# Two transformer layers on one core: norm transposes by DMA, and a reordered first and last stage

## The chip, the cores and the metric

The kernel runs on one core of a Trainium2 chip. The metric is device time in microseconds for one launch. The core has TensorE (matrix products, shown as PE, with its weight loads as PEld), VectorE (DVE), ScalarE (ACT), GpSimd (POOL) and SyncE (SP), which here only issues DMAs. TensorE writes to PSUM[...]; everything else lives in SBUF.

## The reference

The input is 2048 rows of 512 values in bf16. Attention block A and MLP block B are applied twice, with the same weights both times:

```python
x = A_x
x = x + _A_ref(_layernorm(x, axis=-1), A_wqkv, A_wo)
x = x + _B_ref(_layernorm(x, axis=-1), B_w1, B_w2)
x = x + _A_ref(_layernorm(x, axis=-1), A_wqkv, A_wo)
x = x + _B_ref(_layernorm(x, axis=-1), B_w1, B_w2)
return x
```

`_A_ref` is softmax attention without a mask: 32 heads of 16 values, scores scaled by 1/4, each of 2048 queries against 2048 keys, then a product with `wo` (512 x 512). `_B_ref` is `relu(x @ w1) @ w2` with 1792 hidden values. `_layernorm` has no gain or offset; its epsilon is 1e-5.

## The kernel before, in words

**Tiling.** Rows are held as 16 tiles of 128 (`x_t`). A chunk of queries is 512 rows (four tiles) in layer 0. In layer 1 there are two such chunks and then four of 256 rows (`chunks`, L444 to L448), so that less is left after the last one. The last chunk is called LAST, number 5 of layer 1.

**Attention.** Heads have only 16 values, so K and Q lie transposed, four groups of 32 partitions to a tile of heads T. The score matmul at L1302 takes one of the four groups, 32 partitions deep. Each group of 32 holds two heads, and `q_masked` (L624) makes two copies of Q, each with the other head's rows put to zero (the mask `e`). A segment is one chunk, one T and one `e`: sixteen key blocks by four groups. A block is one key block and one group by 512 queries (two key blocks where a chunk has 256). Blocks go in slots of three: a slot fills the three banks of one of the two score tiles `ps_s0` and `ps_s1`, in turn. ScalarE then takes the exponential of the slot in one instruction (L1311), and TensorE multiplies the result with V (L901) into one bank, `ps_o`. V carries a column of ones, so the sums for the softmax come out with the product.

**Pairs.** In some slots the third block does not go to ScalarE but to VectorE (`dve_block`, L991). Two such blocks, two slots apart, are a pair. VectorE makes `exp` from a line (`lin`, L995), the bits of its mantissa (`step`, L1036) and a cube (L1047, L1051), and TensorE multiplies all three with V. ScalarE's instruction then has 1024 columns in place of 1536.

**The planner.** The order of all instructions is made when the program is built. A loop over slots (from L1173) keeps model clocks for TensorE (`now_pe`), VectorE (`now_dve`) and ScalarE (`exp_end`). Other TensorE work is cut into groups of pieces (Q, K, V, Wo, the two MLP products, and the norms' transposes), kept in `work` and `urgent`. `fill_pe` (L307) puts pieces in front of a slot's scores as far as the pace of the stage asks and the model time allows. All of these groups share the one bank `ps_f` outside the first and the last stage. VectorE's tasks lie in `dve_q`, each with a cost and with keys it depends on; `mark` notes when a result is there by the model, with a lag if it comes from GpSimd or a DMA. `run_until` forces what is needed at once. A pair is begun (L1195 to L1220) only if VectorE's queue allows it (L1207, L1208), if the last pair's second half is done, and in layer 0 only if the last V block exists, except for one pair at a time (L1200). Spare TensorE time is filled with repeats of the scores (L1297).

**Norms.** `ln_rows` (L524) makes the tasks: statistics for each tile (L465, L466), then the start of a reciprocal root on VectorE (three small operations, L473 to L480), three Newton steps on GpSimd (L498 to L503), then the apply for each tile (L507). `ln_groups` (L549) makes four TensorE transposes for a tile (L516) into `ps_f`, and VectorE copies the bank to `xnT` (L558). K, V, Q and the first MLP product read `xnT`. There are 16 such norms with 58 tiles. The first norm of all and that of LAST are written out by hand, with the root wholly on VectorE (`ln_rstd` in four parts).

**The end of a segment** (`finish_segment`, L793). The sums are copied from `ps_o` to `u` (L823). For most segments they then go by DMA to a small tile `c` (L828), are inverted (L847), go back (L848), are spread over the partitions by GpSimd's DMA (L850) or a shuffle (L860), and multiplied in (L836). Only the last two segments are divided directly from `u` (`direct`, L869), with the shuffle, then a reciprocal (L873) and a product for each 128 rows.

**First stage.** Eighteen dummy products (L1069) run while the first x tiles arrive. Then come the norm, four transposes with copies that alternate between VectorE and ScalarE (L1092), K for T = 0 and Q for T = 0 with their evacuations, and two V blocks, whose copies are on ScalarE (L1116). Products rotate through seven banks, so K falls in bank 1 of `ps_s1`, Q in its bank 2 and the first V block in `ps_f`. The first slot's scores use `ps_s1`.

**Last stage** (from L1340). When the last segment is done, `run_all` finishes the rest of the MLP of chunk LAST-1 but for its first row tile. Then the rows of LAST get x and seven of the eight head pairs' products with Wo (L1368), the last pair's division and product, a copy by ScalarE (L1375), the norm, the transposes, then the MLP with W1 blocks loaded through the four buffers of `w1buf`, and the store. `half_part(0)` (L1402) does the row tile of LAST-1 that had been kept back.

Of the kernel before, what the change touches and what calls it, by code (L numbers as in the profile page):

```python
# [19 lines left out]
EPS = 1e-5  # L20
RSQRT_SEED = 0x5F3759DF
# [3 lines left out]
def kernel(  # L25
# [55 lines left out]
    RSTD_LAG = 5000.0  # L81
    AHEAD = (8.0, 8.0)
# [72 lines left out]
    stats = [sb([P, nc.vector.BN_STATS_DIM], FP32, f"stats{n}") for n in range(2)]  # L155
# [46 lines left out]
    def bank():  # L202
        if ending[0]:
            bank_no[0] += 1
            return (ps_f[:], ps_s[0][:, 0, :], ps_s[1][:, 0, :])[bank_no[0] % 3]
        if not wide[0]:
            return ps_f[:]
        n = bank_no[0] % 7
        bank_no[0] += 1
        in_bank[0] = (2, 0) if n == 6 else (n // W, n % W)  # L210
        if n == 6:
            return ps_f[:]
        return ps_s[n // W][:, n % W, :]
# [247 lines left out]
    def ln_stats(tag, tt, i):  # L461
        if tag not in ln_seq:
            ln_seq.append(tag)
        st = stats[i % 2]
        nc.vector.bn_stats(out=st[:], in_=x_t[tt][:])  # L465
        nc.vector.bn_aggr(out=mv[ln_n(tag)][:, i, :], in_=st[:])  # L466

    def ln_rstd(tag, part):

        n = ln_n(tag)  # L470
        a, y, t1 = va_[n], ya_[n], ta_[n]
        if part == 0:
            nc.vector.tensor_scalar(  # L473
                out=a[:], in0=mv[n][:, :, 1], scalar1=EPS, scalar2=None, op0=ALU.add
            )
            nc.vector.tensor_scalar(
                out=t1[:].bitcast(I32), in0=a[:].bitcast(I32), scalar1=1, scalar2=None,
                op0=ALU.logical_shift_right,
            )
            nc.vector.tensor_scalar(  # L480
                out=y[:].bitcast(I32), in0=t1[:].bitcast(I32), scalar1=-1.0,
                scalar2=float(RSQRT_SEED), op0=ALU.mult, op1=ALU.add,
            )
            return
        nc.vector.scalar_tensor_tensor(
            out=t1[:], in0=y[:], scalar=-0.5, in1=y[:], op0=ALU.mult, op1=ALU.mult
        )
        nc.vector.tensor_mul(out=t1[:], in0=t1[:], in1=a[:])
        nc.vector.scalar_tensor_tensor(
            out=y[:], in0=t1[:], scalar=1.5, in1=y[:], op0=ALU.add, op1=ALU.mult  # L490
        )

    def ln_newton(tag):

        n = ln_n(tag)
        a, y, t1 = va_[n][:], ya_[n][:], ta_[n][:]
        for _ in range(3):
            nc.gpsimd.tensor_mul(out=t1, in0=y, in1=y)  # L498
            nc.gpsimd.tensor_mul(out=t1, in0=t1, in1=a)
            nc.gpsimd.tensor_scalar(  # L500
                out=t1, in0=t1, scalar1=-0.5, scalar2=1.5, op0=ALU.mult, op1=ALU.add
            )
            nc.gpsimd.tensor_mul(out=y, in0=y, in1=t1)  # L503
# [20 lines left out]
    def ln_rows(tag, tt, n, i):  # L524

        if tag not in ln_seq:
            ln_seq.append(tag)
        at_tag = ln_seq.index(tag)
        prev = ln_seq[at_tag - 1]
        rows_of_prev = chunks[prev[1:]][1]  # L530
        before_that = ln_seq[at_tag - 2] if at_tag > 1 else None
        old = each(chunks[before_that[1:]][1], "xn", before_that) if at_tag > 1 else []
        if ("st", tag, i) not in made:
            task(830, lambda: ln_stats(tag, tt + i, i), [("st", tag, i)], old)
        if i == n - 1:

            def rstd():
                ln_rstd(tag, 0)
                ln_newton(tag)
                mark(("rs", tag, 3), lag=RSTD_LAG)  # L540

            task(500, rstd, [("rs", tag, 3)], each(n, "st", tag) + old)
            for k in range(n):
                task(
                    325, lambda k=k: ln_apply(tag, tt + k, k), [("xn", tag, k)],
                    [("xT", prev, k)] * (k < rows_of_prev) + [("rs", tag, 3)],
                )

    def ln_groups(tag, dst, at_column, n, war):  # L549
        groups = []  # L550
        for i in range(n):

            def piece(i=i):
                pt = ln_transpose(tag, i)

                def fin():
                    a = at_column + i * P
                    nc.vector.tensor_copy(out=dst[:, :, a : a + P], in_=pt)  # L558
                    mark(("xnT", tag, i))

                put_evac(342, fin)

            groups.append(
                group([(1.3, piece)], [("xT", tag, i), ("xnT", tag, i)], [("xn", tag, i)] + war)
            )
        return groups
# [91 lines left out]
    def load_w1(n):  # L658

        if n < len(chunks) * NF:  # L660
            ft = n % NF
            nc.sync.dma_start(
                out=w1buf[n % NW1][:],
                in_=B_w1[:, ft * P : (ft + 1) * P].rearrange("(c p) f -> p c f", p=P),
            )
            mark(("w1", n), "pe", 4000.0)
# [65 lines left out]

    def rest_of_chunk(l, j):

        b = before(l, j)
        xj, a, w = columns(l, j)
        n = w // P
        war_h = each(chunks[b][1], "z", *b) if b else []
        work[0:0] = [o_group(l, j, i) for i in range(n)] + ln_groups(
            ("ln2", l, j), xnT[xj], a, n, []  # L740
        )
        gs = [h_group(l, j, ft, war_h) for ft in range(0, NF, QS // w)]
        gs += [z_group(l, j, i) for i in range((l, j) == (1, LAST - 1), n)]
        if l == 0:
            gs += ln_groups(("ln1", 1, j), xnT[j], 0, TPC, [])
            gs.append(k_group(1, 0, j))
            gs += [v_group(1, kb) for kb in range(j * TPC, (j + 1) * TPC)]
            gs += [k_group(1, T, j) for T in range(1, 4)]
        return gs
# [43 lines left out]
    def finish_segment(sg, last):  # L793
# [37 lines left out]
        musts.append((77 + 1.045 * width, now_pe[0] + PE_TO_DVE, copy))  # L831
# [37 lines left out]
        def direct(i):  # L869
            if i == 0:  # L870
                spread()
            a = i * P
            nc.vector.reciprocal(out=r[:, a : a + P], in_=r[:, a : a + P])  # L873
            mul(a, P)
# [36 lines left out]
    def v_ready(sg, t):  # L911

        found = []
        done = [
            (p, x) for p in pairs if p["sg"] is sg
            for x in p["mms"] if x[4] in made and at([x[4]], "pe") <= t
        ]
        slots = [s for s in pend if s["ready"] <= t]
        for g in range(4):
# [3 lines left out]
                for s in slots for x in s["blocks"] if x[0] is sg and x[2] == g  # L923
# [42 lines left out]
    def force_v():  # L966
# [6 lines left out]
        if not found:  # L973
            run_until(next(x[4] for p in pairs if p["sg"] is sg for x in p["mms"]))
            found = v_ready(sg, 1e18)
        for home, _, _ in found:
            for s in pend:
                if s["blocks"] is home:
                    t = max(t, s["ready"])
            for p in pairs:  # L980
                if p["mms"] is home:
                    t = max(t, *(at([f[1][4]], "pe") for f in found if f[0] is home))
# [89 lines left out]
    idle_matmuls(18)  # L1072
# [12 lines left out]
    for part in range(4):  # L1085
        ln_rstd(tag, part)
# [3 lines left out]
    for i in range(TPC):  # L1090
        pt = ln_transpose(tag, i)
        copy = nc.scalar.copy if i % 2 else nc.vector.tensor_copy  # L1092
        uses(copy(out=xnT[0][:, :, i * P : (i + 1) * P], in_=pt), in_bank[0], "xnT")
        mark(("xnT", tag, i))
        idle_matmuls(1)
    for i in range(3):
# [13 lines left out]
    b = plain(q_mms(0, 0, 0))  # L1110
    for e in range(2):
        uses(q_masked(0, b, e), in_bank[0])
    mark(("q", 0))
    for kb in range(2):
        b = plain(v_mms(kb))
        uses(nc.scalar.copy(out=v_out(0, kb), in_=v_in(b)), in_bank[0])  # L1116
        mark(("v", 0, kb))
    work.extend(v_group(0, kb) for kb in range(2, TPC))
    for j in range(1, NQS):
# [4 lines left out]
        work.extend(ln_groups(tag, xnT[j], 0, TPC, []))  # L1124
# [40 lines left out]
    now_pe[0] = 12000.0  # L1165
    now_dve[0] = 13400.0
    exp_end = {-1: 13600.0, 0: 13600.0}
# [5 lines left out]
    while units:  # L1173
# [155 lines left out]
        for sg, kb, g in now:  # L1329
            run_until(("v", sg["l"], kb))  # L1330
# [9 lines left out]
    while seg_at[0] < len(segs):  # L1340
        force_v()
        run_dve(0.0, musts)
    ending[0] = True
    run_all()
    ending[0], wide[0] = False, True
# [22 lines left out]
    for i in rows:  # L1368
        add(banks[i], ident[:], x_t[tt + i][:], True, False)
        for t in range(NT - 1):  # L1370
            add(banks[i], ot[t][:, part(i)], wo[:, t // 2, :], False, False)
    for i in rows:
        last_steps[0](i)
        add(banks[i], ot[NT - 1][:, part(i)], wo[:, (NT - 1) // 2, :], False, True)
# [3 lines left out]
    for step in range(4):  # L1378
        ln_rstd(tag, step)
    for i in rows:  # L1380
        ln_apply(tag, tt + i, i)

# [26 lines left out]
    for ft in range(NF + 1):  # L1409
        if ft < NF:  # L1410
            n = (l * NQS + j) * NF + ft
            b = more[ft % 4]
            for c in range(NDC):
                add(
                    b, w1buf[n % NW1][:, c, :], xnT[NQS - 1][:, c, at_column : at_column + width],
# [10 lines left out]
            load_w1(n + NW1)  # L1426
# [6 lines left out]
    for i in rows:  # L1433
        copy = nc.vector.tensor_copy if i % 2 else nc.scalar.copy
        uses(copy(out=x_t[tt + i][:], in_=at_bank(banks[i])), banks[i])
        nc.sync.dma_start(
# [32 lines left out]
```

The softmax here doesn't subtract the row's maximum and nothing guards it: scores larger than these inputs give would overflow.

## Time and profile before

| | before |
|---|---|
| time, median of 3 runs | 1613.98 us (1613.9 to 1615.33) |
| span of the profiled run | 1611.5 us |
| ScalarE, VectorE, TensorE busy | 97%, 93%, 90% |
| exponentials (L1311) | 1366, 1554.8 us |
| of these with 1024 columns | 662 |
| pairs on VectorE (L1047) | 331 |
| first exponential starts, last one ends | 16.81 us, 1577.8 us |
| copies of transposes (L558) | 58, 24.3 us |
| W1 loads | 140 of 128 KB |

A line of the groups of instructions has the line of the kernel, the engine, the operation, the tile written and the tiles read, the shapes and the number; after the bar come the busy time and the mean of one in ns; after the next bar, how long the engine had been idle before them, and what ended most of that. TensorE overlaps its products, so sums of its durations overstate its load. VectorE's instructions overlap a little too: the next one often starts some 0.1 us before the recorded end of the one before.

### The profile page before, as it was taken

The page shows a single profiled execution, that of the slowest core. Times are in us where ns is not written, and L with a number is a line of the kernel's source. Part 1 is how long each engine was busy: PE and PEld are TensorE (multiplying, and loading weights), DVE is VectorE, ACT ScalarE, POOL GpSimd, SP SyncE. Part 2 cuts the span into 40 slices and gives each one's busy share as a digit, 9 for nine tenths or more (in the row PEclk, how much of TensorE's full clock was granted, in tenths as well). Part 3 has the DMA queues.
Part 4 walks back from the last instruction along what each step waited for, and adds up shares of the span by engine and source line. Part 5 has one row for each costly group of instructions (what it writes and reads, how often), then busy time and mean ns, then how long its engine had stood idle before and what let it go on. Part 6 is the DMA issues. An engine that isn't in the chain of part 4 may idle for free.

```text
span 1611.5 us, 35252 instructions
## 1 busy us (share of the span) xinstructions
PE 1451.6 (90%) x14667; PEld 508.9 (32%) x14863; DVE 1496.8 (93%) x3007; ACT 1566.0 (97%) x1387; POOL 93.8 (6%) x279
## 2 busy tenths in 40 slices
PE   8888888999989999899998998888989999899997
PEld 3222222322222222222222222222333333344444
DVE  7669999999999999999898998999999999999994
ACT  6999999999999999999999999999999999999993
POOL 2000001001010011000100000001001010010100
PEclk9999999999999999999999999999999999999999
DMA  5000000210002100021000100000210111121223
GB/s 164 1 1 2 2 2 10 46 28 12 5 18 45 21 15 9 12 47 25 9 1 17 31 1 1 2 3 9 44 30 16 26 29 36 22 48 36 47 46 73
DMA packets 113889, 39.97 MB, mean 25 GB/s; under 512 B 103328, under 2 KB 111264, under 8 KB 113728
## 3 DMA queue, kind: packets, MB, share of 16 engines
q1 hardware_dynamic: 101696, 26.21, 7.1%
q0 software_dynamic: 10688, 10.18, 3.4%
q8 instruction: 116, 1.90, 0.5%
q10 hardware_dynamic: 1344, 1.31, 0.2%
q14 instruction: 45, 0.37, 0.1%
HBM read 24.38 MB, written 2.10 MB: 16 GB/s over the span
## 4 chain that ended last, share of the span: by engine, by line
ACT 78%; PE 11%; DVE 7%; issue 3%; DMA 1%; ACTq 0%; DVEq 0%
ACT e L1311 78%; PE ps_s L1302 4%; PE ps_o L901 3%; PE ps_f L434 3%; DVE lin L995 2%; DVE step L1036 1%; PE ps_s L1365 1%; DVE cube L1047 1%; DVE cube L1051 1%; DVE stats L465 0%; DVE ht L682 0%; DVE q L625 0%; DVE ot L836 0%; DVE x L708 0%; DMA c<-u 0%
## 5 line engine op out<-in xcount | busy, mean ns | idle before, releaser
L1311 ACT ACTIVATE e<-ps_s 128x1024 bf16<-128x1024 f32 (+1 forms) x1366 | 1554.8, 1367 | 6.6 <-PE ps_s L1302 4.7
L1302 PE MATMUL ps_s<-q,ktp 32*128 32x512 bf16 (+1 forms) x6060 | 601.2, 341 | 106.7 <-ACT e L1311 84.7
L901 PE MATMUL ps_o<-e,vaug 128*32 128x512 bf16 (+1 forms) x4284 | 494.7, 345 | 11.3 <-DVE u L823 4.8
L995 DVE TENSOR_SCALAR lin<-ps_s 128x512 int16<-128x512 f32 x662 | 452.6, 686 | 35.8 <-PE ps_s L1302 30.4
L1302 PEld LDWEIGHTS <-ktp 32*128 32x128 bf16 x6060 | 189.9, 91 | 504.5 <-issue 375.6
L1036 DVE TENSOR_SCALAR step<-lin 128x1024 int16<-128x1024 int16 x662 | 262.9, 420 | 3.3 <-PE ps_o L901 0.6
L901 PEld LDWEIGHTS <-vaug 128*32 128x32 bf16 x6004 | 161.5, 94 | 302.2 <-issue 291.5
L1047 DVE TENSOR_TENSOR cube<-step 128x1024 f16<-128x1024 bf16 x331 | 225.9, 685 | 2.7
L1051 DVE TENSOR_TENSOR cube<-cube,lin 128x1024 bf16<-128x1024 f16 x331 | 225.5, 682 | 0.0
L901 PE MATMUL ps_o<-step,vaug 128*32 128x512 bf16 (+1 forms) x836 | 143.2, 340 | 0.3 <-issue 0.3
L901 PE MATMUL ps_o<-cube,vthird 128*32 128x512 bf16 (+1 forms) x788 | 138.2, 337 | 0.6 <-issue 0.3
L901 PE MATMUL ps_o<-lin,vaug 128*32 128x512 bf16 (+1 forms) x836 | 127.4, 338 | 4.1 <-DVE u L823 2.8
L434 PE MATMUL ps_f<-xnT,w 128*128 128x512 bf16 (+1 forms) x446 | 116.9, 345 | 5.6 <-issue 2.5
L434 PE MATMUL ps_f<-w,ht 128*128 128x512 bf16 x334 | 104.8, 384 | 5.6 <-issue 4.3
L850 POOL DMA_DIRECT2D r<-u x52 | 37.5, 721 | 1165.9 <-DVE step L1036 424.3
L434 PE MATMUL ps_f<-xnT,wqkv 128*128 128x512 bf16 (+1 forms) x288 | 82.3, 359 | 6.4 <-issue 2.5
L682 DVE TENSOR_SCALAR ht<-ps_f 128x512 bf16<-128x512 f32 x103 | 70.7, 687 | 3.2 <-PE ps_f L434 3.0
L434 PE MATMUL ps_f<-wo,ot 128*128 128x512 bf16 x206 | 65.4, 384 | 3.0 <-issue 1.9
L625 DVE TENSOR_SCALAR q<-ps_f,qmask 128x512 bf16<-128x512 f32 (+1 forms) x102 | 64.8, 661 | 3.1 <-PE ps_f L434 3.0
L434 PEld LDWEIGHTS <-w 128*128 128x128 bf16 x504 | 39.1, 97 | 60.0 <-issue 50.6
L836 DVE SCALAR_TENSOR_TENSOR ot<-u,mask,r 128x512 bf16<-128x512 f32 (+2 forms) x82 | 51.3, 627 | 1.1
L901 PEld LDWEIGHTS <-vthird 128*32 128x32 bf16 x788 | 39.8, 95 | 32.8 <-issue 30.1
(91 smaller groups left out, 609.8 us busy)
## 6 DMA issues: line engine op xcount, KB each, us to landing
w<-in_B_w_dram SPq DMA_DIRECT2D x140, 128.0 KB
r<-u POOLq DMA_DIRECT2D x25, 256.0 KB, 7.1
r<-u POOLq DMA_DIRECT2D x27, 128.0 KB, 4.5
out_dram<-x SPq DMA_DIRECT2D x16, 128.0 KB
x<-in_A_x_dram SPq DMA_DIRECT2D x14, 128.0 KB
w<-in_B_w_dram SPq DMA_DIRECT2D x1, 1792.0 KB
wqkv<-in_A_wqkv_dram ACTq DMA_DIRECT2D x2, 512.0 KB
c<-u SPq DMA_DIRECT2D x48, 8.0 KB
```

Source lines behind the costliest of these rows:

```text
L434: nc.tensor.matmul(out, lhsT, rhs, start=i % k == 0, stop=i % k == k - 1)
L625: return nc.vector.tensor_scalar(out=qbuf[n % 2][e][:, 0:w], in0=b, scalar1=qmask[e][:, 0:1], scalar2=None, op0=ALU.mult,)
L682: nc.vector.tensor_scalar(out=out, in0=sums, scalar1=0.0, scalar2=None, op0=ALU.max)
L836: nc.vector.scalar_tensor_tensor(out=ot[t][:, at_column + a : at_column + a + w], in0=u[:, a : a + w], scalar=mask[e][:, 0:1], in1=r[:, a ...
L850: nc.gpsimd.dma_start(out=r[:, 0:width], in_=bass.AP(tensor=sums.tensor, offset=sums.offset, ap=[list(sums.ap[0]), [0, 32], [1, width]],),)
L901: nc.tensor.matmul(ps_o[32 * g : 32 * g + 32, 0 : sg["w"]], values[:, 4 * sg["T"] + g, 2 * e : 2 * e + 32], rhs, start=g not in sg["begun" ...
L995: first = nc.vector.tensor_scalar(out=lin[which][:, half * QS : (half + 1) * QS], in0=src, scalar1=EXP_BIAS, scalar2=0.0, op0=ALU.add, op1 ...
L1036: nc.vector.tensor_scalar(out=stair, in0=line, scalar1=keep, scalar2=put, op0=ALU.bitwise_and, op1=ALU.bitwise_or,)
L1047: (609, lambda: nc.vector.tensor_mul(out=power, in0=mantissa, in1=mantissa)),
L1051: (609, lambda: nc.vector.tensor_mul(out=power.bitcast(BF16), in0=power, in1=line.bitcast(BF16))),
L1302: nc.tensor.matmul(b[:, a : a + sg["w"]], kt[32 * g : 32 * g + 32, kc : kc + P], qbuf[sg["n"] % 2][sg["e"]][32 * g : 32 * g + 32, 0 : sg[" ...
L1311: ex = nc.scalar.activation(out=eb[:, 0 : place[m]], in_=b[:, 0 : place[m]], func=ACTF.Exp, scale=1.0 / (LOG2E * UNIT),)
```

## The change: what it does and what it is for

**Transposes by DMA.** A norm's apply is followed by a DMA from SyncE's queue that transposes the tile from `xnbuf` straight to `xnT`. TensorE's transposes and VectorE's copies are gone for all 16 planned norms. The planner counts the result as there `X_LAG` = 4000 ns after the apply. The purpose is to take work from VectorE, TensorE and the bank `ps_f`.

**Norm arithmetic.** The statistics are gathered first and aggregated with the seed of the root. The seed takes two VectorE operations for three. Where the root is wholly on VectorE, a cubic step with a gain and one Newton step take the place of three Newton steps.

**First stage.** There are 24 dummy products for 18. The first two copies of transposes go to ScalarE and the last two to VectorE. Two tiles of the next norm get their statistics ahead of Q, where it was three. The first V block goes between Q's two masks and is copied by VectorE; the second becomes planned work. The slot loop no longer forces the V blocks of a slot: a product with V is picked only when its V block exists, by two new tests in `v_ready` and `force_v`. The loop's starting clocks are new numbers.

**Last stage.** The last segment's sums are spread and divided straight from `ps_o`, ahead of the leftover MLP of chunk LAST-1, and the rows' products with Wo follow at once. The W1 blocks of the last chunk are loaded ahead: four in `w1buf` and ten in buffers of layer 0's K that are no longer in use. The last stores go from two queues.

The diff, cut to its core:

```diff
@@ finish_segment
-        musts.append((77 + 1.045 * width, now_pe[0] + PE_TO_DVE, copy))
+        if last:
+            sums_wait[0] -= 1
+        else:
+            musts.append((77 + 1.045 * width, now_pe[0] + PE_TO_DVE, copy))
...
         def direct(i):
+            source = ps_o if last else u
             if i == 0:
-                spread()
+                nc.vector.stream_shuffle(
+                    out=r[:, 0:width], in_=source[:, 0:width], mask=[lane] * 32
+                )
@@ ln_seed, in place of the first part of ln_rstd
+        for i in range(rows):
+            nc.vector.bn_aggr(out=mv[n][:, i, :], in_=stats[n][:, i, :])
+        nc.vector.tensor_scalar(
+            out=va_[n][:, 0:rows], in0=mv[n][:, 0:rows, 1], scalar1=EPS, scalar2=gain,
+            op0=ALU.add, op1=ALU.mult,
+        )
+        nc.vector.tensor_scalar(
+            out=ya_[n][:, 0:rows].bitcast(I32), in0=va_[n][:, 0:rows].bitcast(I32), scalar1=-0.5,
+            scalar2=float(RSQRT_SEED), op0=ALU.mult, op1=ALU.add,
+        )
@@ ln_root, in place of the other parts
+        ln_seed(tag, rows, GAIN)
+        a, y, t1 = va_[n][:, 0:rows], ya_[n][:, 0:rows], ta_[n][:, 0:rows]
+        stt = nc.vector.scalar_tensor_tensor
+        nc.vector.tensor_mul(out=t1, in0=y, in1=y)
+        nc.vector.tensor_mul(out=t1, in0=t1, in1=a)
+        stt(out=t1, in0=t1, scalar=-10.0 / 3.0, in1=t1, op0=ALU.add, op1=ALU.mult)
+        stt(out=y, in0=t1, scalar=5.0, in1=y, op0=ALU.add, op1=ALU.mult)
+        stt(out=t1, in0=y, scalar=-0.5 / GAIN, in1=y, op0=ALU.mult, op1=ALU.mult)
+        nc.vector.tensor_mul(out=t1, in0=t1, in1=a)
+        stt(out=y, in0=t1, scalar=1.5, in1=y, op0=ALU.add, op1=ALU.mult)
@@ ln_rows, in place of ln_groups
+            def apply(k):
+                kind, l, j = tag
+                xj, a, _ = columns(l, j) if kind == "ln2" else (j, 0, QS)
+                ln_apply(tag, tt + k, k)
+                a += k * P
+                nc.sync.dma_start_transpose(out=xnT[xj][:, :, a : a + P], in_=xnbuf[k][:])
+                mark(("xT", tag, k), lag=X_LAG)
+                mark(("xnT", tag, k), lag=X_LAG)
@@ rest_of_chunk
+        if (l, j) == (1, LAST - 2):
+            for ft in range(NF):
+                home = (
+                    w1buf[((l * NQS + LAST) * NF + ft) % NW1] if ft < NW1
+                    else (kt01 + kt2)[(ft - NW1) // 2][:, ft % 2, :].rearrange(
+                        "p (c f) -> p c f", c=NDC
+                    )
+                )
...
@@ first stage
-    idle_matmuls(18)
+    idle_matmuls(24)
...
-        copy = nc.scalar.copy if i % 2 else nc.vector.tensor_copy
+        copy = nc.vector.tensor_copy if i > 1 else nc.scalar.copy
...
-    b = plain(q_mms(0, 0, 0))
-    for e in range(2):
-        uses(q_masked(0, b, e), in_bank[0])
+    q_bank = plain(q_mms(0, 0, 0))
+    at_q = in_bank[0]
+    uses(q_masked(0, q_bank, 0), at_q)
+    b = plain(v_mms(0))
+    uses(nc.vector.tensor_copy(out=v_out(0, 0), in_=v_in(b)), in_bank[0])
+    mark(("v", 0, 0))
+    uses(q_masked(0, q_bank, 1), at_q)
     mark(("q", 0))
...
-    now_pe[0] = 12000.0
-    now_dve[0] = 13400.0
-    exp_end = {-1: 13600.0, 0: 13600.0}
+    now_pe[0] = 13160.0
+    now_dve[0] = 14500.0
+    exp_end = {-1: 12600.0, 0: 13600.0}
@@ slot loop
-        for sg, kb, g in now:
-            run_until(("v", sg["l"], kb))
@@ last stage
+    while seg_at[0] < len(segs):
+        force_v()
+        run_dve(0.0, musts)
     for i in rows:
         last_steps[0](i)
+    for i in rows:
+        first_part(i)
         add(banks[i], ot[NT - 1][:, part(i)], wo[:, (NT - 1) // 2, :], False, True)
         uses(nc.scalar.copy(out=x_t[tt + i][:], in_=at_bank(banks[i])), banks[i], "x")
     for i in rows:
         ln_stats(tag, tt + i, i)
-    for step in range(4):
-        ln_rstd(tag, step)
+    ln_root(tag, n_rows)
     for i in rows:
         ln_apply(tag, tt + i, i)
+    ending[0], wide[0] = True, False
+    run_all()
+    ending[0], wide[0] = False, True
```

## The prediction

> **What bounds the kernel now.** I read the page from the top: shares of the engines, groups of instructions, then the waits of each engine, the groups by shape, the busy time by stretch, and the chain and the timeline of the two ends.
>
> ```profile
> PE 1451.6 (90%) x14667; PEld 508.9 (32%) x14863; DVE 1496.8 (93%) x3007; ACT 1566.0 (97%) x1387; POOL 93.8 (6%) x279
> ...
> L1311 ACT ACTIVATE e<-ps_s 128x1024 bf16<-128x1024 f32 (+1 forms) x1366 | 1554.8, 1367 | 6.6 <-PE ps_s L1302 4.7
> ...
> L558 DVE COPY xnT<-ps_f 128x512 bf16<-128x512 bf16 x58 | 24.3, 419 | 3.6 <-PE ps_f L516 3.2
> ```
>
> ScalarE takes 1366 exponentials and waits 6.6 us for them in the whole run. The first starts at 16.81 us, the last ends at 1577.8. So the time is three pieces: 16.8 before, 1561 of a full ScalarE, 33.7 after. The middle shrinks only if ScalarE gets less work. By shape:
>
> ```profile
> L1311 ACT ACTIVATE e<-ps_s 128x1536 bf16<-128x1536 f32 x703 | 1052.1, 1573 | 4.5 <-PE ps_s L1302 2.8 <-PE ps_o L901 1.2
> L1311 ACT ACTIVATE e<-ps_s 128x1024 bf16<-128x1024 f32 x662 | 717.7, 1148 | 2.1 <-PE ps_s L1302 1.9 <-PE ps_o L901 0.2
> ```
>
> The number of slots is fixed (4096 blocks of 512 columns, three a slot). In 662 slots the third block is taken by VectorE instead, and ScalarE's call is 1573 - 1148 = 425 ns shorter. Two such blocks are one pair, worth 0.85 us. So VectorE's free time is the currency of the middle. How much of it is there:
>
> ```profile
> 20.00:118.00 98.00, 85.87 (x659) 28.92 (x664) 68.33 (x138) 97.51 (x78) 7.68 (x36) 1.00 0.05 14
> 118.00:1578.00 1460.00, 1324.16 (x13776) 459.13 (x13953) 1401.08 (x2791) 1454.14 (x1288) 83.73 (x208) 1.00 0.10 21
> ```
>
> (Columns: stretch, length, then PE, PEld, DVE, ACT, POOL.) From 118 us VectorE is at 96%: a pair more needs work taken off it. Before, it is at 70%, because L1200 lets only one pair live until the sixteenth V block is made (its copy starts at 111.16 us). TensorE is not scarce: among its waits, the scores stand 84.7 us for ScalarE to free their banks.
>
> The end, from the chain:
>
> ```profile
> 1577.39 0.87 PE ps_o L901 x20
> ...
> 1580.16 2.98 PE ps_s L434 x13
> ...
> 1583.24 0.70 DVE x L708
> ...
> 1583.98 3.84 PE ps_s L1365 x17
> ...
> 1593.06 0.73 PE ps_s L516 x8
> ...
> 1598.39 3.27 DMA w<-in_B_w_dram
> ```
>
> TensorE first finishes the MLP of the chunk before, VectorE adds it, and only then do the last head's division, Wo and the norm run, with TensorE idle for 0.85 us at 1583.1 and 1.75 us before 1593.06. Later one W1 load is waited for.
>
> [...]this trace has no DMA transpose, and its TensorE ones take 221 ns each as recorded. [...]the move back of the reciprocals is issued at 395.93 and releases GpSimd at 398.25, 2.3 us.
>
> ```profile
> 395.93 0.53 SPq L848 DMA_DIRECT2D u<-c  x1
> ...
> 398.25 0.78 POOL L850 DMA_DIRECT2D r<-u  x1 [1.28 <-DMA u<-c]
> ```
>
> **The change, part by part.**
> *Transposes by DMA.* 58 tiles of 16 norms lose their four TensorE transposes and the copy at L558. A copy is 419 ns as recorded, but the next instruction starts 0.33 us after it (66.34 to 66.67), so it frees 58 x 0.335 = 19.4 us of VectorE. The shorter seed (two operations for three, 0.2 us apart) frees 16 x 0.2 = 3.2. The statistics move without growing. Together 22.6 us. A pair is, from start to start in the stretch 416 to 419 us, 2 x 0.60 (line) + 2 x 0.34 (step) + 2 x 0.60 (cube) = 3.1 us. That is 7 pairs, 7 x 0.85 = **6.0 us** off ScalarE. The planner puts them in by itself, since L1208 counts queued VectorE work. TensorE's extra products hide in its waiting.
>
> *Early stage.* Twelve transposes with their turn of the single bank ps_f (1.1 to 1.3 us each at 35 to 40 us) lie ahead of the sixteenth V block. Without them it should come 5 to 12 us sooner. The rate of pairs goes from one in some 11 us to one in 4, so 1 to 2 pairs more: I take **0.9 us**, bounds 0 and 1.7.
>
> *The new wait.* H, K and V products now wait for a landing, and stand in TensorE's order ahead of scores. The planner counts 4.0 us from the apply (X_LAG). Below: 0.53 issue and 2.3 landing, as above. [...]The nearest large row, the 256 KB broadcast, lands in a median of 7.1 us. I take some 3 to 4 us, as the four tiles are issued in a row and may overlap; late landings then cost 0.1 us for each of 16 norms, **1.5 us lost**. Behind a transpose on SyncE's queue wait the small DMAs of the divisions (78 c<-u, 78 u<-c) and W1 loads; VectorE waits for c at L847 but has slept there only 0.2 us in all, and 156 x 0.55 us of issue leave the queue mostly empty, so this is at nothing unless an issue takes well over 1 us. The wait of VectorE's apply for the old tile (xnbuf) is a norm old: nothing.
>
> *Head.* The root has nine small steps for twelve, 0.6 us; the copies start on ScalarE, which is idle from 3.2 us, not behind VectorE's applies; the last xnT copy should end near 11.3 us, not 12.13. But the first K weights were loaded at 11.64 after 0.26 us of waiting for a DMA, so K starts near 11.7, not 12.18. Then Q needs 8 products (1.9 us), its first mask 0.75, the V copy 0.69 and the second mask 0.75 on VectorE: 16.0 us. Q lies in the third bank of ps_s1, which the first scores overwrite, so they start at 16.0, not 16.37 behind the two V groups that are now later. Gain **0.4 us**; 2 if the scores do not stand for the second mask. The six extra dummies (0.2 us each) end at 8.5, before the first apply.
>
> *End.* The last sums are spread and divided from PSUM at once, from 1578.4: shuffle 0.44, then per row 0.95 + 0.35. Row 2 is ready at 1581.5, its Wo product at 1582.4, ScalarE's copy at 1583.1; stats to 1583.9, the root 9 x 0.2, the first normed row at 1586.5 (1593.0 before). TensorE meanwhile: 16 products and two identities to 1582.4, the two H groups (2.0), 14 z products (3.0), the half part (3.2): 1590.8. So TensorE sets the transposes at 1590.8, **2.3 us** earlier: what it had idled, less a short stop for row 1. The kept weights remove the stop at 1601 (steps of 1.34 us against 0.87): **0.5**. Stores from two queues: **0.2**. W1's last loads move to dead K buffers in an earlier stage, hidden.
>
> Sum: 6.0 + 0.9 - 1.5 + 0.4 + 3.0 = 8.8 us, so **1605.2 us**.
>
> **Rivals.**
> *Late landings (slower).* Tiles land 2 us after the planned time or later, and c<-u stands behind four transposes. TensorE waits in order, with one slot of scores ahead (1.15 to 1.57 us), so ScalarE loses 1 us or so at each of 16 norms, and some 78 divisions lose a few tenths: 16 + 15 us, against 10.3 gained: 1635; with half of the losses 1619. For it: nothing in the trace shows such a DMA[...]. Against: between apply and H there is mostly Q or K work to do, and 4 us is 1.7 times the measured plain landing.
> *The freed VectorE time buys nothing.* Pairs are held by their other conditions (own segment still to come, a pair per three slots). Then head and end remain, 3.4 - 1.5: 1612. For it: VectorE still waits 30.4 us for scores at L995. Against: 96% busy, and 331 pairs in 1366 slots are well under one in three.
> *More than counted.* The gate opens 12 us sooner, ps_f's turns no longer hold VectorE's casts (11.8 + 7.2 us of waits at L611 and L575), ten to eleven pairs, head 2: 1614 - 9 - 1.7 - 2 - 3 + 0.5 = 1599.
>
> **Chances.** Forecast 0.57, late landings 0.14, nothing bought 0.15, more 0.14. Faster by over 0.2% (under 1610.8): 0.57 + 0.14 + two fifths of the third case = 0.77; same 0.09; slower 0.14. The range takes the forecast with its unknowns, "more" down to 1598, and the weak end of the others up to 1616; beyond are the late landings and a few in a hundred below.
>
> **What the profile after would show.** Right: L558's group gone, the 1024-column calls near 678 and ScalarE's sum lower by 6 to 7 us with its waits still under 10; transposes landing within 4 us; the first exponential near 16.4; some 30 us from the last exponential to the end. Wrong: TensorE waiting for a DMA that writes xnT, ScalarE's waits for scores above 15 us, L847 waiting for c, or a pair count unchanged. The forecast falls if SyncE's issue of a transpose takes well over 1 us, since all that I put at nothing hangs on that queue.

## The result, and the profile after

| | before | after |
|---|---|---|
| time, median (lowest to highest), 4 runs each | 1613.99 us (1613.9 to 1615.33) | 1630.51 us (1629.59 to 1634.52) |
| ratio to before, 95% interval | | 1.0105 [1.0087, 1.0123] |
| span of the profiled run | 1611.5 us | 1629.3 us |
| first exponential starts | 16.81 us | 15.95 us |
| from there to the end of the last one | 1561.0 us | 1586.7 us |
| from there to the end | 33.7 us | 26.6 us |
| exponentials with 1024 columns; pairs | 662; 331 | 670; 335 |

The kernel became 1.05% slower; 1605.2 us was forecast. Both ends gained, 0.9 and 7.1 us. The middle lost 25.7 us. The page says which kind of time that is:

```profile
PE 1450.0 (89%) x14408; PEld 495.9 (30%) x14597; DVE 1485.5 (91%) x2950; ACT 1562.9 (96%) x1383; POOL 93.3 (6%) x279
...
L1339 ACT ACTIVATE e<-ps_s 128x1536 bf16<-128x1536 f32 (+1 forms) x1366 | 1554.2, 1360 | 35.5 <-PE ps_s L1330 33.7
```

ScalarE's work is what it was (1554.2 against 1554.8 us), but it now waits 35.5 us where it waited 6.6, nearly always for scores (2.98 us of this lie before the first exponential, against 0.40 before). TensorE in turn waits for a DMA that writes `xnT`. The waits of each engine give the number of times and the longest one:

```profile
ACT e L1339 <- PE ps_s L1330: 33.7, 28, 5.7
...
PE ps_f L436 <- DMA xnT<-xn: 19.4, 8, 5.3
```

So the loss is not spread over the 16 norms. Four stops hold most of it: ScalarE stands still for 3.98 us before 410.85, 4.04 before 487.32, 5.67 before 615.87 and 4.83 before 810.91, together 18.5 us, or 23.1 us with the shorter waits that follow each stop within 5 us. The timeline of the changed kernel around the longest one (start, length, engine, line, then in brackets how long the engine had been idle and what released it; SPq is SyncE's queue):

```profile
602.48 0.70 POOL L860 DMA_DIRECT2D r<-u  x1 [0.28 <-issue]
...
603.29 9.59 SPq L551 DMA_TRANSPOSE xnT<-xn  x4
...
604.43 0.40 DVE L510 TENSOR_SCALAR xn<-x,mv,ya 128x512 bf16<-128x512 bf16 x1
...
614.27 0.58 PE L436 MATMUL ps_f<-xnT,wqkv 128*128 128x512 bf16 x1 [5.34 <-DMA xnT<-xn]
...
615.22 0.61 PE L1330 MATMUL ps_s<-q,ktp 32*128 32x512 bf16 x3 [0.36 <-issue]
...
615.87 1.02 ACT L1339 ACTIVATE e<-ps_s 128x1024 bf16<-128x1024 f32 x1 [5.67 <-PE ps_s L1330]
```

GpSimd starts the broadcast of a segment's reciprocals (`r<-u`, 256 KB). VectorE applies the norm, and SyncE issues its four transposes, which take 9.59 us to issue. The last apply ends at 604.83, so by the planner's count the last tile is there at 608.8; the K product that needs it starts at 614.27, and the scores behind it in TensorE's order at 615.22. The chain of work that ended last goes the same way: SyncE's queue at 610.29, then 2.47 us from the start of the last issue to its landing. Where no broadcast is near, four issues take 5.13 us, 1.2 us each:

```profile
668.06 5.13 SPq L551 DMA_TRANSPOSE xnT<-xn  x4
```

At the other three large stops a broadcast is in flight too; it starts 0.2, 0.8 and 1.7 us after the first of the four issues, where here it starts 0.8 us before. The records of the DMA packets show what happens meanwhile. From 606 to 609 us (packets, MB, and the time that the packets took as a share of 16 engines):

```profile
q1 hardware_dynamic: 17, 0.00, 52.3%
q0 software_dynamic: 36, 0.15, 25.5%
```

`q1` has SyncE's DMAs and `q0` GpSimd's. For three microseconds next to nothing of the transposes is moved while the broadcast's packets of 4 KB run, and the 17 small packets of `q1` still take 52.3% of the engines' time, so most of that share looks like packets that stand. It is the same at the other stops: `q1` moves under 0.01 MB from 404 to 406, 479 to 482 and 803 to 806 us. Once the broadcast has landed, from 610 to 614 us, the transposes move:

```profile
q1 hardware_dynamic: 1674, 0.40, 94.7%
```

The busy time by stretch (PE, PEld, DVE, ACT, POOL, then granted TensorE clock, DMA share, GB/s) shows one thing more:

```profile
610.00:614.00 4.00, 0.00 (x0) 0.00 (x0) 0.28 (x1) 0.20 (x1) 0.00 (x0) 0.59 0.96 104
614.00:618.00 4.00, 3.37 (x16) 0.75 (x17) 1.69 (x3) 1.53 (x2) 0.00 (x0) 0.50 0.00 0
```

TensorE comes out of the stop at a granted clock of 0.50, where it was 1.00 from 602 to 610 us: products of 512 columns take 0.61 us for 0.39, and ScalarE waits another 0.60 and 0.72 us at the next slots.

### The profile page after: what moved, and what is told of

The parts are those of the page before. It is cut to its first block, busy times and chain, and to the rows that moved or that the text cites. A ratio compares the mean times of both kernels' runs of the same rounds, so it can differ in the third digit from the quotient of the medians.

```text
span 1629.3 us, 34816 instructions
## 1 busy us (share of the span) xinstructions
PE 1450.0 (89%) x14408; PEld 495.9 (30%) x14597; DVE 1485.5 (91%) x2950; ACT 1562.9 (96%) x1383; POOL 93.3 (6%) x279
## 3 DMA queue, kind: packets, MB, share of 16 engines
q10 hardware_dynamic: 1488, 1.44, 0.3%
## 4 chain that ended last, share of the span: by engine, by line
ACT 72%; PE 12%; DVE 12%; DMA 3%; issue 2%; SPq 0%; ACTq 0%; DVEq 0%
ACT e L1339 72%; PE ps_s L1330 4%; PE ps_f L436 4%; DVE lin L1025 3%; PE ps_o L918 3%; DVE step L1066 2%; DVE cube L1077 1%; DVE cube L1081 1%; DMA xnT<-xn 1%; PE ps_s L1390 1%; DVE q L619 1%; DVE ht L676 1%; DMA wqkv<-in_A_wqkv_dram 0%; DVE xn L510 0%; DMA r<-u 0%
## 5 line engine op out<-in xcount | busy, mean ns | idle before, releaser
L1339 ACT ACTIVATE e<-ps_s 128x1536 bf16<-128x1536 f32 (+1 forms) x1366 | 1554.2, 1360 | 35.5 <-PE ps_s L1330 33.7
L1025 DVE TENSOR_SCALAR lin<-ps_s 128x512 int16<-128x512 f32 x670 | 457.8, 686 | 48.4 <-PE ps_s L1330 43.3
L1330 PEld LDWEIGHTS <-ktp 32*128 32x128 bf16 x6003 | 186.4, 91 | 518.3 <-issue 389.5
L1066 DVE TENSOR_SCALAR step<-lin 128x1024 int16<-128x1024 int16 x670 | 266.5, 420 | 3.7 <-PE ps_o L918 0.6
L436 PE MATMUL ps_f<-xnT,w 128*128 128x512 bf16 (+1 forms) x457 | 120.9, 347 | 11.7 <-DMA xnT<-xn 5.5
L436 PE MATMUL ps_f<-w,ht 128*128 128x512 bf16 x350 | 109.6, 384 | 4.4 <-issue 3.8
L436 PE MATMUL ps_f<-xnT,wqkv 128*128 128x512 bf16 (+1 forms) x292 | 86.3, 370 | 19.8 <-DMA xnT<-xn 13.9
L846 DVE SCALAR_TENSOR_TENSOR ot<-u,mask,r 128x512 bf16<-128x512 f32 (+1 forms) x78 | 49.7, 638 | 1.8 <-DMA r<-u 0.9
```

Of the source, the lines that this page charges most:

```text
L436: nc.tensor.matmul(out, lhsT, rhs, start=i % k == 0, stop=i % k == k - 1)
L846: nc.vector.scalar_tensor_tensor(out=ot[t][:, at_column + a : at_column + a + w], in0=u[:, a : a + w], scalar=mask[e][:, 0:1], in1=r[:, a ...
L1025: first = nc.vector.tensor_scalar(out=lin[which][:, half * QS : (half + 1) * QS], in0=src, scalar1=EXP_BIAS, scalar2=0.0, op0=ALU.add, op1 ...
L1066: nc.vector.tensor_scalar(out=stair, in0=line, scalar1=keep, scalar2=put, op0=ALU.bitwise_and, op1=ALU.bitwise_or,)
L1330: nc.tensor.matmul(b[:, a : a + sg["w"]], kt[32 * g : 32 * g + 32, kc : kc + P], qbuf[sg["n"] % 2][sg["e"]][32 * g : 32 * g + 32, 0 : sg[" ...
L1339: ex = nc.scalar.activation(out=eb[:, 0 : place[m]], in_=b[:, 0 : place[m]], func=ACTF.Exp, scale=1.0 / (LOG2E * UNIT),)
```

## The experiments

All ratios are to the kernel before on the same chip, with 95% intervals; they are not the quotients of the medians shown. Times of single spots are from the profiled runs. Diffs are against the kernel after, unless it says before.

**One part undone: e1_pe_transposes.** The transposes of the planned norms go back to TensorE, with VectorE's copies.

```diff
-                nc.sync.dma_start_transpose(out=xnT[xj][:, :, a : a + P], in_=xnbuf[k][:])
-                mark(("xT", tag, k), lag=X_LAG)
-                mark(("xnT", tag, k), lag=X_LAG)
...
+    def ln_groups(tag, dst, at_column, n, war):
...
+        work[0:0] = [o_group(l, j, i) for i in range(n)] + ln_groups(
+            ("ln2", l, j), xnT[xj], a, n, []
+        )
```

> The changed kernel with one part undone: the planned norms transpose on TensorE and copy on VectorE as before; the new first and last stage and the norm arithmetic stay. Theory A (late landings: TensorE stands in order for DMA transposes that the planner counts as there 4.0 us after the apply): ScalarE's waits for scores fall from 33.7 us to under 10, and the time is 1603 to 1609 us. Theory B (the new plan of V blocks, starting clocks and stages holds ScalarE up, the DMA only changes pairs): the waits stay above 20 us and the time above 1620.

Measured 1623.95 us, 1.0075 [1.0055, 1.0094]: the time that theory B named. ScalarE waits 24.7 us in all, 14.5 of it for scores, which lies between the two. Taken alone, this run speaks for B. But the timeline of this kernel shows another kind of stop than the kernel after has:

```profile
105.45 0.58 PE L519 MATMUL ps_f<-ident,xn 128*128 128x128 bf16 x4 [0.52 <-DVE xnT L561]
...
106.55 1.86 PE L436 MATMUL ps_f<-xnT,wqkv 128*128 128x512 bf16 x4 [0.52 <-DVE xnT L561]
...
109.91 1.02 ACT L1352 ACTIVATE e<-ps_s 128x1024 bf16<-128x1024 f32 x1 [4.53 <-PE ps_s L1343]
```

Transposes, their copies and the K product come in a row with no scores between them. By the program this is what `run_until` does with a group whose result is needed at once; the trace shows the row, not the reason. The other large stop, 5.12 us before 1216.84, follows ten products of the MLP in a row. So undoing a part also draws a new order of the whole middle, and that order may hold a new stop. A comparison of two differently planned kernels can't be read as the price of the part.

**How large that effect is: e7_before_rstd_lag and e9_before_rstd_lag_4500.** The kernel before, with one planner constant changed. Only the order changes, no operation.

```diff
-    RSTD_LAG = 5000.0
+    RSTD_LAG = 5500.0
```

> The kernel before with one planner constant moved: the root of a norm is counted as there 5.5 us after its start in place of 5.0. No instruction is added or taken away, only the order changes. It shows how much a new order costs by itself. If the plan adapts smoothly (what the forecast took for granted): within 2 us of before. If any new order brings forced groups and stalls as in the two undoings (e1, e2): 8 to 15 us slower, 1621 to 1628.

> The kernel before with the planner's lag for a norm's root at 4.5 us in place of 5.0, the other way from e7. The plan has two forced groups where before has three and e7 five. If stalls come with forced groups: within 4 us of before, either side. If any change of the order costs 10 us: 1622 or more.

Measured 1623.78 us, 1.006 [1.0045, 1.0075] with 5500, and 1611.86, 0.999 [0.9977, 1.0003] with 4500. The first has a stop of 5.1 us from 1207.3, behind ten products of the MLP in a row as in e1; the kernel before has none over 1.3 us. A plan alone is worth 10 us. The parts of the change are worth less than that, so the experiments that decide are those that hold the order.

**The lag: e2_lag_10us.**

```diff
-    X_LAG = 4000.0
+    X_LAG = 10000.0
```

> The changed kernel with one constant changed: the planner counts a DMA transpose as there 10.0 us after the apply in place of 4.0. Theory A: products that read xnT are placed later, TensorE's waits for the transposes fall from 23 us to under 3, ScalarE's waits under 10, time 1601 to 1607. Theory B, or a rival C (the transposes cost by loading the DMA engines and SyncE's queue, whatever the planner knows, or the delay only moves the crowding): above 1615.

Measured 1628.78 us, 1.0102 [1.0077, 1.0127]. The time is that of theory B and rival C. No wait of TensorE for `xnT` is left, but ScalarE waits 33.3 us all the same, 22.4 of it for scores and 9.5 for products with V. The order is again another one, and its two largest stops have two causes. The 4.25 us before 830.75 follow products with Wo and a V block in a row. The 4.15 us before 1416.97 come from SyncE's queue:

```profile
1406.57 6.51 SPq L741 DMA_DIRECT2D ktp<-in_B_w_dram  x10
...
1415.09 0.20 DVE L857 RECIPROCAL c<-c 128x8 f32<-128x8 f32 x1 [5.21 <-DMA c<-u]
```

The ten W1 loads that the change issues ahead stand in front of a division's `c<-u`, VectorE waits 5.21 us for it, and the scores wait for VectorE. The prediction had these loads as hidden. In the kernel after they are: VectorE waits 0.8 us for `c` in the whole run. The wait for `xnT` was taken away and the time was not.

**The DMA transposes alone: e4_dma_only.** The kernel before with the transposes by DMA and nothing else of the change.

```diff
+                nc.sync.dma_start_transpose(out=xnT[xj][:, :, a : a + P], in_=xnbuf[k][:])
+                mark(("xT", tag, k), lag=X_LAG)
+                mark(("xnT", tag, k), lag=X_LAG)
...
-        work.extend(ln_groups(tag, xnT[j], 0, TPC, []))
```

> The kernel before with one part of the change alone: the planned norms transpose by DMA with the lag of 4.0 us. Theory A: TensorE waits 20 us or more for the landings, ScalarE loses 25 to 30 us, time 1635 to 1643. Theory B (the rest of the plan is at fault): near 1612.

Measured 1628.0 us, 1.0098 [1.0083, 1.0113]. TensorE waits 17.3 us for `xnT` (longest 6.9), ScalarE 26.0 us for scores (longest 7.4). The time is below what theory A had (1635 to 1643), but the pattern is the one of after: the waits for `xnT` come with this part, without the new first and last stages.

**No broadcasts, planned anew: e3_no_broadcast.** All segments are spread by VectorE's shuffle.

```diff
-        quick = sg["load"] is not None or ended[l, j] == NT
+        quick = True
```

> The changed kernel with GpSimd's 52 broadcasts of the reciprocals replaced by VectorE's shuffle, as the last segments already have it. If the long issues (3 to 4 us instead of 1.2) come from the broadcast being in flight (theory A1), all issues take about 1.2 us, TensorE's waits for xnT fall from 23 us to 5 to 9, ScalarE's to about 12, and with some 31 us more on VectorE (5 pairs fewer) the time is about 1612 to 1620. If the long issues have another source (theory A2: four transposes in a row fill the queue by themselves), waits stay near 23 us and the time goes to 1634 or more.

Measured 1618.0 us, 1.0023 [1.0008, 1.0038]. The mean issue of a transpose falls to 1.28 us (1.62 after), TensorE's waits for `xnT` to 3.5 us. The plan is again another one, and VectorE has 52 shuffles more.

**No broadcasts, the same order: e6_no_bcast_same_order.** The order of after is kept and the 52 broadcasts are left out; `r` holds ones, so the division of those segments is missing.

```diff
+    for r in rbuf:
+        nc.gpsimd.memset(r[:], 1.0)
...
-                nc.gpsimd.dma_start(
-                    out=r[:, 0:width],
...
```

> The changed kernel with every instruction in its order, but GpSimd's 52 broadcasts of the reciprocals are left out (r holds ones from the start, so this leaves out the division in those segments). Theory A1 (the broadcast in flight makes the transposes' issues long): all issues take 1.2 us, the last of four tiles lands some 7 us after its apply's start, TensorE's waits for xnT fall from 23 us to 3 to 6, and the time is 1604 to 1611. Theory A2 (four transposes in a row are slow by themselves): waits stay above 15 us and the time above 1620.

Measured 1610.22 us, 0.9972 [0.996, 0.9984]. Its waits:

```profile
ACT e L1333 <- PE ps_s L1324: 11.3, 14, 3.0
...
PE ps_f L438 <- DMA xnT<-xn: 5.6, 5, 2.0
```

In the two traces the instructions of VectorE, ScalarE and TensorE's weight loads stand in the same order, one for one. With that order, taking away 52 DMAs of another queue takes away 14 of TensorE's 19.4 us and two thirds of ScalarE's waits. The middle of the profiled run, the fastest of e6, is 1561.8 us for 1586.7. The late landings at the four large stops are caused by the broadcasts. (Without any broadcast some issues still take up to 2.27 us, so something else stretches them too, but less.)

**Is it the transposing? e5_plain_copy.** The order of after, with each transpose replaced by a plain copy of the same 128 KB; the transposition is left out.

```diff
-                nc.sync.dma_start_transpose(out=xnT[xj][:, :, a : a + P], in_=xnbuf[k][:])
+                nc.sync.dma_start(
+                    out=xnT[xj][:, :, a : a + P], in_=xnbuf[k][:].rearrange("p (c f) -> p c f", c=NDC)
+                )
```

> The changed kernel with every instruction in its order, but each of the 58 DMA transposes is a plain copy of the same 128 KB from the same queue to the same place (so the normed rows are not transposed: this leaves out the transposition). Theory A (late landings alone hold the changed kernel up): an issue takes some 0.5 us and lands 2 to 3 us later, within the planned 4.0 us; TensorE's waits for xnT fall from 23 us to under 3, ScalarE's from 33.7 to under 10, and the time is 1601 to 1608, what the plan promises. Theory B (the plan as such, or DMA traffic of any kind beside the scores, is at fault): waits above 20 us, time above 1620.

Measured 1627.77 us, 1.0087 [1.0053, 1.0121]; TensorE waits 15.1 us for `xnT`. (With these other data the profiled run had a mean clock of 0.884 and was the longest of the four; the others had 0.98 and more.) A copy alone issues in 0.59 to 0.66 us, half of a transpose's 1.22. But near a broadcast that starts at 607.84, in the timeline of this kernel:

```profile
608.66 6.82 SPq L551 DMA_DIRECT2D xnT<-xn  x4
...
617.70 1.01 PE L436 MATMUL ps_f<-xnT,wqkv 128*128 128x512 bf16 x2 [3.42 <-DMA xnT<-xn]
```

Four copies take 6.82 us to issue, and the product starts only after the broadcast has landed, at 615.7. The expectation that a copy would come through was wrong: a plain copy beside this broadcast is held back too, so the transposing is not needed for the loss.

**A landing time that counts the queue: e10_step_lag.** The four tiles of a norm are counted as there 4, 5, 6 and 7 us after their applies. The broadcasts stay.

```diff
-                mark(("xnT", tag, k), lag=X_LAG)
+                mark(("xnT", tag, k), lag=X_LAG + 1000.0 * k)
```

> The changed kernel with the planner told of the queue: tile k of a norm is counted as there 4.0 + 1.0 k us after its apply, in place of 4.0 for all. Broadcasts stay. The plan has no forced group (as the changed kernel's). If the issues standing in a row on SyncE's queue were the larger part of the loss: TensorE's waits for xnT fall from 23 us to under 8, time 1606 to 1612. If the broadcasts in flight are the larger part (theory A1): waits of 12 us or more stay, time 1618 to 1628.

Measured 1616.28 us, 1.0015 [1.0003, 1.0026], between the two expectations. TensorE waits for `xnT` twice, 5.2 us in all, which is what the first expectation had; ScalarE waits 20.0 us for scores. Yet broadcasts and transposes still meet: the four issues take 8.36, 9.43 and 8.54 us at the norms near 399, 593 and 786 us. So a late landing alone costs little if the product that needs it stands later in the order. The loss took both, the landing held back by a broadcast and the one flat lag of 4.0 us, as far as two plans can be compared.

**A repair: e8_shuffle_near_norms.** The order of after; the nine segments whose broadcast would lie near a norm's transposes use VectorE's shuffle instead. Nothing is left out.

```diff
+            norm_near = now_dve[0] - moved[0] < 4000.0 or any(
+                k[0] == "xn" for t in dve_q for k in t["makes"]
+            )
+            if norm_near and not quick:
+                by_shuffle.add(n)
+            elif not quick:
...
-            if quick:
+            if quick or n in by_shuffle:
```

> The changed kernel with every planned instruction in its order; only in the nine segments whose division falls beside a norm's transposes, GpSimd's broadcast is replaced by VectorE's shuffle (nine more shuffles of 0.6 us, which the planner is not told of). Nothing is left out of the computation. Theory A1 (a broadcast in flight holds the transposes back, and this is the changed kernel's whole loss): all issues near 1.2 us, TensorE's waits for xnT fall from 23 us to about 5, ScalarE's waits for scores from 34 to about 12, time 1606 to 1612, faster than before. If the nine shuffles collide with lin, up to 1615. If A1 is wrong: above 1620.

Measured 1610.51 us, 0.9977 [0.9968, 0.9985]: faster than both kernels. The order is that of after, but for nine shuffles more on VectorE. Its waits, and the transposes of the same norm as in the timeline of after:

```profile
ACT e L1347 <- PE ps_s L1338: 15.6, 22, 3.0
...
PE ps_f L436 <- DMA xnT<-xn: 5.9, 5, 2.1
```

```profile
591.71 5.60 SPq L551 DMA_TRANSPOSE xnT<-xn  x4
...
598.65 0.58 PE L436 MATMUL ps_f<-xnT,wqkv 128*128 128x512 bf16 x1 [1.16 <-DMA xnT<-xn]
```

From the first issue to the product it is 6.9 us here and was 11.0 us (603.29 to 614.27). By pieces of the profiled run: head 15.8 us, middle 1567.5, end 26.2.

**Both repairs: e11_step_lag_and_shuffle.**

> Both mendings: the lag of 4.0 + 1.0 k us, and the shuffle in place of the broadcast where a norm's transposes are near (as in e8). Theory A1 and a plan without forced groups: TensorE's waits for xnT under 3 us, ScalarE's for scores 8 to 14 us, time 1604 to 1610, faster than e8's 1610.5 or level with it. If new orders cost 10 us whatever they are: 1618 or more.

Measured 1611.08 us, 0.9961 [0.9941, 0.9982]; no wait for `xnT` is left that the profile lists, and ScalarE waits 11.6 us for scores. The time is 1.1 us above the expected range, and level with e8 within the intervals.

## Why the prediction was wrong, point by point

**The new wait: the step that failed.** The prediction took a landing "some 3 to 4 us, as the four tiles are issued in a row and may overlap; late landings then cost 0.1 us for each of 16 norms", 1.5 us in all: an estimate, from other DMAs than transposes. The issues do not overlap: 1.22 us each, one after the other, so the last tile lands some 7 us after the first issue even undisturbed (in e8 its product starts 6.9 us after it). With a broadcast in flight it is 11 us (603.29 to 614.27). The loss is then not 16 times a little but four times 4 to 6 us, each with TensorE at a clock of 0.50 after it, because the K or MLP product stands where the planner's 4.0 us put it. The same order without the broadcasts (e6), or with nine of them moved to VectorE (e8), has the loss back. The prediction's sign of danger, an issue "well over 1 us", was met beside a broadcast (up to 4.05 us; alone it is 1.22). But what it had hung on that sign, VectorE's waits for `c`, came to 0.8 us in all. Its lower bound for a landing also names the issue of 0.53 us beside the 2.3 us from 395.93 to 398.25, which already contain it.

**What was overlooked.** The broadcast was in the prediction, as a row of 7.1 us that bounds a landing, but not as something that is in flight at that very moment. That the two meet has a reason in the program: a norm's applies and a segment's division both follow from the end of a segment. That the two queues hang on each other is shown by e6, where 52 DMAs fewer on GpSimd's took 14 of TensorE's 19.4 us of waits for SyncE's transposes. The bytes were not shared evenly: from 606 to 609 us SyncE's DMAs moved under 0.01 MB beside 0.15 MB of the broadcast. The prediction had only looked at what stands behind SyncE's own queue.

**The late-landings rival** had the mechanism: "TensorE waits in order, with one slot of scores ahead". It had a us at each norm and a few tenths at each division. The divisions lost nothing to speak of (0.8 us), and the losses are few and long.

**Pairs.** Seven were forecast from 22.6 us of VectorE's time. Four came, 4 x 0.84 = 3.4 us by the start-to-start times of ScalarE's calls. Two of them are the early stage's: the copy of the sixteenth V block starts at 102.98 us for 111.16, and seven pairs have begun their cube by 118 us where it was five, as forecast. So the freed time of the middle brought two. VectorE's busy time fell by 11.3 us (1496.8 to 1485.5), so about half of what was freed was left free. What held the further pairs back was not tested. VectorE's time alone does not set their number: with the work unchanged, another plan gives 330 (e7) or 332 (e9) for 331. ScalarE's busy time fell by 0.6 us only. A call of 1536 columns in before is 1573 ns as recorded and 1339 ns from start to start when the next follows at once. Each wait ends that overlap of two calls, 1573 - 1339 = 0.23 us, and ScalarE waits for scores 28 times, not 14; that explains most of the difference, but was not tested.

**Head.** K's products started at 11.32 us (11.7 forecast), the scores at 15.51 after 1.44 us for Q's second mask, as said; the gain is 0.9 us, not 0.4.

**End.** 3.0 us were forecast, 7.1 came. In the timeline of after, the last row tile of chunk LAST-1 gets its MLP result before the last exponential has ended, so nothing of it is left to do:

```profile
1600.74 1.94 ACT L1339 ACTIVATE e<-ps_s 128x1536 bf16<-128x1536 f32 x2 [0.21 <-PE ps_s L1330]
1601.39 0.69 DVE L702 TENSOR_TENSOR x<-x,ps_f 128x512 bf16<-128x512 bf16 x1 [3.95 <-PE ps_s L1330]
...
1611.21 0.72 PE L519 MATMUL ps_s<-ident,xn 128*128 128x128 bf16 x8 [0.61 <-DVE xn L510]
```

Before, that sum stood at 1583.24, 5.4 us behind the last exponential, and the transposes came 15.2 us after it; now it is 8.5 us. This looks like mostly the plan's doing: with the old code of the last stage (e4) the end is 27.9 us, and over all kernels it lies between 26.1 and 35.7. What of the MLP leaves the end is done in the middle.

**The sum.** Head 0.9 and end 7.1 gained, middle 25.7 lost: 26.3 more of ScalarE's waiting, 0.6 less of its work. In e6, where the landings are in time, the same three give 1.2 gained, 0.8 lost, 7.6 gained. That is near the forecast in this one run (1605.3 us), but its median is 1610.2: without the collision the change is worth 0.2 to 0.4%, not the 0.5% forecast.

**What stays open.** Why the transposes move next to nothing for some 3 us beside a broadcast (under 0.01 MB from 606 to 609 us) is not visible: the records have each packet's queue, not its engine. How transposes by DMA and on TensorE compare in plans of equal quality wasn't tried; e1 and e4 differ by less than plans do. That groups forced at once explain the rest of ScalarE's waiting in e1, e2 and e7 is shown for none of them: only rows of products without scores are seen at single stops.

## What to carry to other kernels

Before a step is moved to a DMA whose result is needed by an instruction that others of its engine stand behind (here the K product at 614.27 us, with the scores behind it at 615.22), look for what else is in flight at that moment, not only at what shares its queue: both the consumer and the other big transfer may hang on the same event. Count transfers that are issued in a row with issue time times number, for the last one (here 5.13 us for four transposes of 1.2). And where an order is planned by the program, a part undone draws another order: change the suspected cost with the order held, or measure first how much plans differ by themselves (10 us here).

## What the runs showed of the hardware

- An SBUF-to-SBUF transpose of 128 x 512 bf16 occupies SyncE's queue for 1.22 us, a plain copy of the same size for 0.59 to 0.66. The product that waits for the last of four starts 1.3 to 1.4 us after the end of the last issue, with a broadcast (612.88 to 614.27 in after) or without (e6, e8): what grows is the issues. The issue of a transpose thus takes twice as long, but in the kernel's time no difference is seen: the intervals of e5 (1.0053 to 1.0121) and after (1.0087 to 1.0123) overlap.
- Beside a 256 KB broadcast from GpSimd, issues of 128 KB moves within SBUF stretch to as much as 4.05 us in after (4.60 in e10, 3.10 for the plain copies of e5), against at most 2.27 us with no broadcast in the kernel (e6). At the four large stops of after, the product starts 1.7 to 4.1 us after the broadcast has landed, never before, and for 2 to 3 us of the broadcast's time the transposes move under 0.01 MB.
- TensorE's granted clock is 0.50 for some 3 to 7 us from the product that ends a stop at the four large stops of after (stops of 3.3 to 5.3 us), but it is also 0.50 for some 10 us after a stop of 1.2 us in e8 (598.65 to 608.4 us). What else before that stop may have counted was not tested.
- TensorE's products overlap in the records: in before, the 6060 score products (L1302) have 341 ns each, 6060 x 0.341 = 2066 us in sum, and are 601.2 us of busy time.
